# The opening of a fused attention and gated feed-forward kernel: half-image loads, line sums on other engines, row sums chunk by chunk, a new order

## The chip, the cores and the metric

The kernel runs on one core of one Trainium2 chip. The metric is the device time in microseconds of one execution of the whole program on that core; a lower time is better. Five kinds of work matter here: TensorE (PE in the profile; its weight loads are PEld), VectorE (DVE), ScalarE (ACT), GpSimd (POOL), and the transfers, which are issued by SyncE (SP), ACT or POOL and carried by 16 DMA engines.

## The reference, cut to what matters

```python
B, C, H, W, r = 4, 128, 384, 32, 4                  # four images
kv_pool = kv.reshape(B, H//r, r, W//r, r, C).mean(axis=(2, 4))
k = v = kv_pool.reshape(B, 768, C) @ w_sr           # 768 keys, which are the values too
s = q @ k.T / sqrt(C)                               # q: B x 12288 x 128
a = softmax(s)
x = a @ v                                           # 49152 rows of 128
out = (relu(x @ w_gate) * (x @ w_val)) @ w_out      # 128 -> 1536 -> 128
```

## The kernel before

The 49152 query rows are worked in 96 tiles of 512 rows, 24 tiles to an image. A tile goes through scores against its image's 768 keys (six chunks of 128), exponentials, the weighted sum of values, 24 projections to the 1536 inner columns (12 blocks called `v`, 12 called `g`), and 12 output products `o`. TensorE has eight PSUM banks of 128x512 for all results. The softmax division is done at the very end: the result of a tile is multiplied by the squared inverse of its row sums, which is right because the feed-forward part is of degree two in `x` and `relu` keeps the sign.

The order of all work is written out by hand as lists of words, and each engine executes what is given to it in program order. After the opening, which the list `OPENING` holds, tiles 4 to 95 run in a loop over `FIRST` (the first two rounds), `STEADY` and `DRAIN`. In a round the words `v1`, `y1`, `g1`, `h1` mean: the value projection of block 1 on TensorE, its copy to SBUF on ACT (`keep_value`), the gate projection on TensorE, and relu-and-multiply on VectorE (`gated`). `o1` is an output product, `s0` a score block, `e0` its exponential. The lists don't change for those rounds.

The opening does what has to come before the first round: the keys and values of image 0, and tiles 0 to 3 (the lead tiles) up to their weighted values and row sums, and the 24 projections of tile 0. Its words, each with its function:

- Image 0 comes in as three pairs of chunks. A chunk is 128 pooled pixels, and has four lines, each 128 partitions x 4 pixels x 128 channels in float32. The 16 pixels of a pooled pixel must be summed and the sum turned, channels to partitions. `a3`, `b3`, `c3` add whole lines (`sum_lines`, by the table `SUMS`), `p3` adds pixels 0,1 of that sum to 2,3 (`sum_pixels`), and `T3.0` turns line 0 of chunk 3 by TensorE transposes that add up in one bank: four of 128x128 for a line, two for `T3.p`, which turns what `p3` left. So each line is either summed elsewhere first or costs four transposes of its own.
- `kvT3` copies the bank to SBUF, `pj3` multiplies with `w_sr`, `key3` writes the keys, `vt3` and `val3` make the values from the keys by one transpose and a copy.
- `cast0`, `qt0`, `qT0` turn the queries of tile 0 (cast to float16, four transposes, copy); tiles 4 and 5 are turned by DMA (`qT4`, `qT5`).
- `S2.3` is the score product of tile 2 with chunk 3 and, in the same word, its exponential on ACT (line 345); `V2.3` adds the chunk to the tile's weighted values; `xT2` copies these.
- `U0` and `U1` are the row sums: `lead_sums` multiplies the exponentials with a block of ones for the four lead tiles at once, packed in four column groups (line 432). `U0` does five chunks, `U1` the sixth. `R` turns and inverts them on VectorE, and spreads them with 16 small copies on POOL.
- `v0.5` and `g0.5` are the projections of tile 0, each with its copy, or its relu-and-multiply, in the same word.
- `W0`, `W1`, `wo` are the loads of the feed-forward weights on POOL's queue; `gate22` holds them back until line 2 of chunk 5 is there. After the opening a second such copy (line 699) waits for block 11 of tile 0 before the query load of tiles 8 to 11.

The table `ENGINES` puts a word on ACT (`a`), POOL (`p`) or VectorE (`v`, also the default). A PSUM bank is taken by the next word that needs one in program order, from the bank that was freed longest ago; the instruction then waits for that bank's last reader. In the last eight words only six of the eight banks may be taken, as the rounds have just six for this use. The image and query loads are issued before all this, on SP, with two of the first lines on ACT's queue; the order is that of the calls at lines 592 to 600: pair 0, `w_sr`, queries 0 and 1, line 0 of pair 1, queries 2 and 3, lines 1 to 3 of pair 1, pair 2 (512 KB for each line of a pair), queries 5 and 4.

Of the kernel before, what the change touches and what calls it, by code (L numbers as in the profile page):

```python
# [11 lines left out]
AF = mybir.ActivationFunctionType  # L12
# [4 lines left out]
def kernel(  # L17
# [229 lines left out]
    def line(chunk, dh):  # L247
        return kv_in[0, chunk // 2][dh][:, chunk % 2]
# [88 lines left out]
    aTs, x_banks, x16s, xTs, rinvs = {}, {}, {}, {}, {}  # L337
    hTs, o_banks, o_sbs, vals = {}, {}, {}, {}

    def scores(k, jc):  # L340
        if k not in aTs:
            aTs[k] = work.tile([128, NJC, T], FP16, tag="aT", bufs=AT_BUFS, name="aT")
        s_ps = bank([128, T])
        nc.tensor.matmul(s_ps, kv16[:, k // NST, jc, 0:C], qT_of(k), start=True, stop=True)  # L344
# [79 lines left out]
        xTs[k] = work.tile([128, NS, 128], FP16, tag="xT", bufs=4, name="xT").rearrange("c s p -> c (s p)")  # L424
        copy_on(name, xTs[k], freed(x_banks.pop(k)))

    def lead_sums(chunks):
        if "sums" not in x_banks:
            x_banks["sums"] = bank([128, T])
        for jc in chunks:  # L430
            for k in range(LEAD):
                nc.tensor.matmul(  # L432
                    x_banks["sums"][32 * k : 32 * (k + 1), :], ones, aTs[k][:, jc, :],
                    start=jc == 0, stop=jc == NJC - 1, skip_group_check=True,
                    tile_position=(0, 32 * k),
                )
# [22 lines left out]

    def keep_value(k, fb):  # L460
        vals[k, fb] = work.tile([128, T], FP16, tag="val", bufs=6, name="val")
        (nc.vector.tensor_copy if k < LEAD - 1 and fb == 5 else nc.scalar.copy)(  # L462
            vals[k, fb], freed(proj_banks.pop(("v", k, fb)))
        )

# [126 lines left out]
    kv_load(0, 0, range(r), (nc.sync, nc.scalar))  # L592
    nc.sync.dma_start(w_sr_f32, w_sr)
    q_load_pair(0)
    kv_load(0, 1, range(1))
    q_load_pair(2)
    kv_load(0, 1, range(1, 4))
    kv_load(0, 2)
    q_load_tile(5)
    q_load_tile(4)  # L600
# [19 lines left out]
    freed(idle)  # L620

    gate = const.tile([128, 1], FP32)
    done = set()

    def open_step(word):
        head = "T" if word[0] == "T" else word.rstrip("0123456789.")
        at = [int(x) for x in word[len(head):].split(".") if x] if head != "T" else []
        if head in ("a", "b", "c"):
            j = at[0]
            x, y = SUMS[j][head]  # L630
            sum_lines(word, j, sums[j] if x == "s" else line(j, x), line(j, y))
        elif head == "p":
            sum_pixels(word, at[0])
        elif head == "r":
            c2 = pixels[at[0]]
            add(word, c2[:, 0], c2[:, 0], c2[:, 1])
        elif head == "T":
            j, part = word[1:].split(".")
            turn_add(
                int(j), line(int(j), int(part)) if part.isdigit() else  # L640
                pixels.pop(int(j))[:, 0 : 2 if part == "p" else 1],
            )
        elif head == "kvT":
            turned(word, at[0])
        elif head == "pj":
            project_chunk(at[0])
        elif head == "key":
            keep_keys(word, at[0])
        elif head == "vt":
            turn_chunk_values(at[0])  # L650
        elif head == "val":
            keep_chunk_values(word, at[0])
        elif head == "cast":
            q_cast(at[0])
        elif head == "qt":
# [153 lines left out]
```

## Time and profile before

| | |
|---|---|
| time, median of 3 runs | 1026.08 us (1025.98 to 1026.23) |
| the profiled execution: span from first to last instruction | 1024.5 us (the page gives no other time of it) |
| busy: PE, DVE, ACT, POOL | 1019.4, 861.8, 919.9, 524.8 us |
| opening on PE: first transpose, first word of the first round | 8.07 us, 36.44 us |
| granted TensorE clock | 1.000 |

Times are microseconds from the start of the span. A row of the timeline has the start, the length, engine, line, operation, what it writes and reads, and the count of a run of such instructions; in brackets the idle time ahead of it and what ended that. Matmuls are pipelined, so the length of one row is longer than the distance to the next: start to start is what an engine pays. A table by stage gives the busy time (and instructions) of PE, PEld, DVE, ACT and POOL in each stretch, the granted clock, the DMA share and GB/s.

### The profile page before, as it was taken

The page shows a single profiled execution, that of the slowest core. Times are in us where ns is not written, and L with a number is a line of the kernel's source. Part 1 is how long each engine was busy: PE and PEld are TensorE (multiplying, and loading weights), DVE is VectorE, ACT ScalarE, POOL GpSimd, SP SyncE. Part 2 cuts the span into 40 slices and gives each one's busy share as a digit, 9 for nine tenths or more (in the row PEclk, how much of TensorE's full clock was granted, in tenths as well). Part 3 has the DMA queues.
Part 4 walks back from the last instruction along what each step waited for, and adds up shares of the span by engine and source line. Part 5 has one row for each costly group of instructions (what it writes and reads, how often), then busy time and mean ns, then how long its engine had stood idle before and what let it go on. Part 6 is the DMA issues. An engine that isn't in the chain of part 4 may idle for free.

```text
span 1024.5 us, 17514 instructions
## 1 busy us (share of the span) xinstructions
PE 1019.4 (100%) x5048; PEld 489.5 (48%) x5048; DVE 861.8 (84%) x1432; ACT 919.9 (90%) x1931; POOL 524.8 (51%) x1308
## 2 busy tenths in 40 slices
PE   9999999999999999999999999999999999999998
PEld 5444444444444444444444444444444444444445
DVE  2888888888888888888888888888888888888888
ACT  5999999989999999899999999989999999999986
POOL 3588857344346586544434856654333543343342
DMA  9999999877998999869879899887686987867541
GB/s 330 159 173 184 176 183 159 151 131 120 139 184 168 189 186 164 143 115 146 128 126 211 160 180 194 157 138 134 118 139 108 145 134 119 129 115 123 102 87 45
DMA packets 475312, 153.49 MB, mean 150 GB/s; under 512 B 451536, under 2 KB 465360, under 8 KB 475216
## 3 DMA queue, kind: packets, MB, share of 16 engines
q1 hardware_dynamic: 453184, 126.08, 67.7%
q0 software_dynamic: 21600, 25.19, 15.9%
q10 hardware_dynamic: 432, 1.11, 0.3%
q8 instruction: 40, 0.66, 0.3%
q14 instruction: 56, 0.46, 0.1%
HBM read 53.94 MB, written 26.35 MB: 78 GB/s over the span
## 4 chain that ended last, share of the span: by engine, by line
PE 98%; DMA 1%; ACT 1%; SPq 0%; issue 0%
PE bank_ps L455 24%; PE bank_ps L468 24%; PE bank_ps L496 23%; PE bank_ps L401 12%; PE wide_ps L359 12%; DMA q<-in_q_dram 1%; PE bank_ps L482 1%; PE bank_ps L344 1%; PE bank_ps L418 1%; PE bank_ps L270 0%; PE wide_ps L302 0%; PE bank_ps L284 0%; ACT a L364 0%; ACT val L462 0%; PE bank_ps L432 0%
## 5 line engine op out<-in xcount | busy, mean ns | idle before, releaser
L476 DVE SCALAR_TENSOR_TENSOR hT<-bank_ps,val 128x512 f16<-128x512 f32 x1152 | 727.8, 680 | 105.4 <-PE bank_ps L468 83.7
L462 ACT CAST val<-bank_ps 128x512 f16<-128x512 f32 x1149 | 628.1, 595 | 45.4 <-PE bank_ps L455 24.9
L455 PE MATMUL bank_ps<-xT,wv 128*128 128x512 f16 x1152 | 420.5, 379 | 0.0
L468 PE MATMUL bank_ps<-xT,wg 128*128 128x512 f16 x1152 | 375.9, 379 | 0.0
L496 PE MATMUL bank_ps<-hT,wo 128*128 128x512 f16 x1116 | 348.4, 379 | 0.0
L364 ACT ACTIVATE a<-wide_ps 128x768 f16<-128x768 f32 x368 | 302.0, 821 | 44.0 <-PE wide_ps L359 43.9
L359 PE MATMUL wide_ps<-kv,qT 128*128 128x512 f16 x736 | 179.7, 326 | 0.1
L401 PE MATMUL bank_ps<-aT,kv 128*128 128x512 f16 x552 | 178.9, 379 | 0.0
L496 PEld LDWEIGHTS <-wo 128*128 128x128 f16 x1116 | 109.2, 98 | 131.9 <-issue 0.6
L468 PEld LDWEIGHTS <-wg 128*128 128x128 f16 x1152 | 112.7, 98 | 122.4 <-issue 0.2
L509 POOL TENSOR_TENSOR o_sb<-o_t,scale 128x512 f32<-128x512 f32 x89 | 93.2, 1047 | 145.9 <-issue 128.4
L455 PEld LDWEIGHTS <-wv 128*128 128x128 f16 x1152 | 112.7, 98 | 105.7 <-issue 1.2
L385 POOL COPY scale<-square 32x8 f32<-32x8 f32 x736 | 141.2, 192 | 28.6
L739 POOL DMA_DIRECT2D out_dram<-o_sb x216 | 134.8, 627 | 19.5 <-POOL o_sb L509 13.0
L378 POOL TENSOR_TENSOR square<-inverse 128x8 f32<-128x8 f32 x46 | 9.3, 202 | 255.6 <-DVE inverse L376 249.4
L359 PEld LDWEIGHTS <-qT 128*128 128x128 f16 x736 | 72.0, 98 | 87.1 <-issue 0.4
L409 DVE CAST xT<-bank_ps 128x512 f16<-128x512 f32 x92 | 63.6, 691 | 32.0 <-PE bank_ps L401 32.0
L401 PEld LDWEIGHTS <-kv 128*128 128x128 f16 x552 | 54.0, 98 | 65.1
L364 ACT ACTIVATION_READ_ACCUMULATOR a<-wide_ps 128x1 f32 x368 | 75.9, 206 | 0.0
L504 DVE STREAM_TRANSPOSE o_t<-bank_ps 128x512 f32<-128x512 f32 x93 | 65.4, 703 | 0.0
L144 POOL DMA_DIRECT2D q<-in_q_dram x84 | 46.7, 573 | 0.6 <-PE bank_ps L496 0.4
L237 POOL TENSOR_TENSOR s<-kv_in 128x512 f32<-128x512 f32 x36 | 45.1, 1284 | 0.7
(78 smaller groups left out, 204.9 us busy)
## 6 DMA issues: line engine op xcount, KB each, us to landing
kv_in<-in_kv_dram SPq DMA_DIRECT2D x42, 512.0 KB, 4.7
out_dram<-o_sb SPq DMA_DIRECT2D x177, 64.0 KB, 3.7
out_dram<-o_sb POOLq DMA_DIRECT2D x176, 64.0 KB, 4.2
q<-in_q_dram POOLq DMA_DIRECT2D x84, 128.0 KB, 5.8
aT<-a SPq DMA_TRANSPOSE x184, 4.3
kv_line<-in_kv_dram SPq DMA_DIRECT2D x4, 512.0 KB, 9.7
placed<-blocks SPq DMA_DIRECT2D x9, 128.0 KB, 2.7
kvT<-placed SPq DMA_DIRECT2D x36, 32.0 KB, 2.1
```

Source lines behind the costliest of these rows:

```text
L359: nc.tensor.matmul(s_ps[:, j0 * 128 : j1 * 128], qT, kv16[:, b, j0:j1, 0:C], start=True, stop=True)
L364: nc.scalar.activation(a16s[k][:, s, :], s_banks.pop(s)[:, 0:J], AF.Exp, scale=qk_scale, accum_out=a_sums[k // 2][:, k % 2, s : s + 1],)
L385: nc.gpsimd.tensor_copy(to[32 * b : 32 * (b + 1), :, :, j], squares[k // 2][32 * j : 32 * (j + 1)])
L401: nc.tensor.matmul(x_banks[k], kv16[:, k // NST, jc, C : 2 * C], aT[:, jc], start=first, stop=x_left[k] == 0,)
L455: nc.tensor.matmul(proj_banks["v", k, fb], wv16[:, fb * 128 : (fb + 1) * 128], xTs[k], start=True, stop=True,)
L462: (nc.vector.tensor_copy if k < LEAD - 1 and fb == 5 else nc.scalar.copy)(vals[k, fb], freed(proj_banks.pop(("v", k, fb))))
L468: nc.tensor.matmul(proj_banks["g", k, fb], wg16[:, fb * 128 : (fb + 1) * 128], xTs[k], start=True, stop=True,)
L476: nc.vector.scalar_tensor_tensor(hTs[k][:, fb, :], freed(proj_banks.pop(("g", k, fb))), 0.0, vals.pop((k, fb)), op0=ALU.max, op1=ALU.mult,)
L496: nc.tensor.matmul(o_banks[k], wo16[:, fb, :], hTs[k][:, fb, :], start=fb == 0, stop=fb == NFB - 1)
L504: nc.vector.transpose(o_t, freed(o_banks.pop(k)))
L509: nc.gpsimd.tensor_tensor(to, o_by, scale.to_broadcast([128, NS, 4, 32]), op=ALU.mult)
L739: queue.dma_start(*out_moves.pop())
```

## The change

Six things are changed, all in the opening:

1. The last pair of image 0 is loaded chunk by chunk: `kv_load` gets `half`, and `K4`, `K5` in the new list `LOADS` are four loads of 256 KB each, with rows of 2 KB in place of 4 KB. All other loads keep their order.
2. Lines 0 and 1 of every chunk are summed (`a`), and for chunks 2 to 5 line 2 is added too (`b`). Lines 2 and 3 of chunks 0 and 1 and line 3 of the others are still turned alone. That is 44 transposes of lines and sums in place of 62.
3. The row sums are made chunk by chunk (`U0` to `U5`), in six places of the list.
4. `S` and its exponential become two words (`S`, `E`), and so do `v` and its copy (`y`), `g` and its relu-and-multiply (`h`), so that other words may stand between.
5. `ENGINES`: ACT now has `kvT0`, `key1`, `cast1`, `qT2`, `val2`, `xT1`, `xT2` beside the exponentials and 11 of the 12 copies `y`; POOL has `a1`, `p0`, `b2`, `a4` and the casts of tiles 0, 4 and 5; VectorE has the rest, `y0.0` included.
6. A new `OPENING`, in which the last 12 words are held to six banks; `gate21` in place of `gate22` (line 1 of chunk 5).

```diff
-        key0:a val0:a a1:p kvT1:a key1:a val1:a key2:a val2:a a3:p b3:p p3:p kvT3:a val3:a
-        cast0:a cast1:a qT1:a cast3:a cast4:p cast5:p xT1:a xT3:a
+        cast4:p cast5:p a1:p p0:p kvT0:a cast0:p key1:a cast1:a qT2:a b2:p a4:p val2:a y0.0:v
+        xT1:a xT2:a
     """.split()
     OPENING = """
-        T0.1 T1.3 cast1 T0.3 cast0 T1.2 T0.2 a1 p1 T1.p T0.0 kvT1 kvT0 pj1 qt1 pj0 T2.0 qT1 a3
-        key1 cast3 qt0 cast2 vt1 qT0 key0 S1.1 qt2 qt3 qT2 val1 qT3 S1.0 S0.1 T2.1 S0.0 vt0 val0
-        V1.1 S2.0 b3 c3 S2.1 S3.0 S3.1 T2.2 V0.1 T2.3 V1.0 kvT2 V2.1 V0.0 p3 gate22 W0 W1 cast4
-        qT4 wo cast5 qT5 pj2 V2.0 T3.p T5.0 key2 vt2 kvT3 val2 pj3 key3 S0.2 T5.1 vt3 val3 S2.3
-        a4 S0.3 S1.2 S2.2 T5.2 V0.2 S3.2 b4 V2.3 T5.3 V0.3 c4 S1.3 kvT5 S3.3 pj5 p4 T4.p V1.2
-        key5 kvT4 V1.3 S0.5 pj4 key4 S2.5 vt5 val5 V2.2 S0.4 vt4 val4 S2.4 V0.5 V3.0 S1.4 V0.4
-        S3.4 xT0 S1.5 V2.5 V2.4 S3.5 xT2 v0.5 g0.5 U0 v0.2 U1 v0.0 R g0.2 v0.3 V1.4 V3.1 g0.0
-        v0.1 v0.4 V1.5 g0.3 v0.9 v0.11 g0.4 g0.9 V3.4 v0.8 v0.10 g0.1 xT1 g0.8 V3.5 v0.7 g0.11
-        V3.3 v0.6 V3.2 g0.10 xT3 g0.7 g0.6
+        a0 a1 p0 T1.2 p1 T0.2 T0.p T1.p T1.3 T0.3 kvT1 pj1 kvT0 pj0 cast0 key1 cast1 vt1 key0
+        qt0 val1 vt0 qt1 qT0 qT1 S0.1 S0.0 val0 S1.1 E0.1 S1.0 cast3 E0.0 V0.1 cast2 qt3 E1.1
+        V0.0 qt2 qT3 E1.0 V1.1 a3 S3.1 qT2 S3.0 V1.0 a2 E3.0 S2.1 S2.0 b3 b2 E3.1 V3.0 E2.1 p3
+        V3.1 E2.0 T3.p p2 T3.3 U0 T2.p kvT3 U1 pj3 a4 T2.3 key3 vt3 S1.3 kvT2 S0.3 val3 pj2
+        E1.3 b4 T4.3 E0.3 S3.3 key2 V1.3 p4 vt2 E3.3 S1.2 V0.3 a5 gate21 W0 W1 T4.p val2 S2.2
+        E1.2 S3.2 kvT4 V3.3 b5 E2.2 S0.2 pj4 V1.2 E3.2 p5 T5.3 key4 E0.2 T5.p S0.4 S3.4 kvT5
+        S2.4 E0.4 pj5 V3.2 E2.4 key5 vt4 U2 V0.2 val4 E3.4 S0.5 S3.5 vt5 E0.5 V0.4 V3.4 val5
+        S1.5 E3.5 V0.5 S2.5 E1.5 S2.3 xT0 V3.5 S1.4 E2.3 V1.5 xT3 v0.0 E2.5 v0.5 g0.3 y0.0 g0.0
+        y0.5 g0.5 U5 h0.0 E1.4 v0.1 v0.3 U3 y0.1 h0.5 U4 v0.6 y0.3 V2.0 cast4 qT4 wo cast5 qT5
+        R g0.6 v0.7 y0.6 V2.5 V1.4 y0.7 v0.8 h0.3 V2.4 V2.3 xT1 g0.7 h0.6 g0.1 y0.8 v0.2 g0.8
+        h0.7 v0.9 y0.2 V2.1 h0.8 v0.4 y0.9 g0.2 v0.11 h0.1 g0.11 y0.4 g0.4 v0.10 y0.11 h0.2
+        V2.2 g0.9 g0.10 y0.10 h0.4 xT2 h0.9 h0.11 h0.10
     """.split()
+    LOADS = "P0 w Q0 P1.0 Q2 P1.1 P1.2 P1.3 K4 K5 q5 q4".split()
...
-    SUMS = [{}, {"a": [0, 1]}, {}, {"a": [0, 1], "b": ["s", 2], "c": ["s", 3]}, {"a": [0, 1], "b": ["s", 2], "c": ["s", 3]}, {}]
+    SUMS = [{'a': [0, 1]}, {'a': [0, 1]}, {'a': [0, 1], 'b': ['s', 2]}, {'a': [0, 1], 'b': ['s', 2]}, {'a': [0, 1], 'b': ['s', 2]}, {'a': [0, 1], 'b': ['s', 2]}]
...
+            if half is not None:
+                own = slice(half * r * C, (half + 1) * r * C)
+                to, line_rows = to[:, own], line_rows[:, :, own]
+            queues[dh % len(queues)].dma_start(to, line_rows)
...
-        nc.scalar.activation(aTs[k][:, jc, :], freed(s_ps), AF.Exp, scale=qk_scale)
+
+    def exponentials(k, jc):
+        nc.scalar.activation(
+            aTs[k][:, jc, :], freed(score_ps.pop((k, jc))), AF.Exp, scale=qk_scale
+        )
...
-    def lead_sums(chunks):
+    def lead_sums(jc):
         if "sums" not in x_banks:
-            x_banks["sums"] = bank([128, T])
-        for jc in chunks:
-            for k in range(LEAD):
-                nc.tensor.matmul(
...
+            x_banks["sums"], x_count["sums"] = bank([128, T]), 0
+        x_count["sums"] += 1
+        for k in range(LEAD):
+            nc.tensor.matmul(
+                x_banks["sums"][32 * k : 32 * (k + 1), :], ones, aTs[k][:, jc, :],
+                start=x_count["sums"] == 1, stop=x_count["sums"] == NJC, skip_group_check=True,
+                tile_position=(0, 32 * k),
+            )
...
-        (nc.vector.tensor_copy if k < LEAD - 1 and fb == 5 else nc.scalar.copy)(
+        on_vector = ENGINES.get(f"y0.{fb}", "a") == "v" if k == 0 else k < LEAD - 1 and fb == 5
+        (nc.vector.tensor_copy if on_vector else nc.scalar.copy)(
...
-        elif head == "v":
-            value_proj(*at)
-            keep_value(*at)
-        elif head == "g":
-            gate_proj(*at)
-            gated(*at)
+        elif head in ("v", "y", "g", "h"):
+            {"v": value_proj, "y": keep_value, "g": gate_proj, "h": gated}[head](*at)
...
-        usable[0] = 8 if at < len(OPENING) - 8 else 6
+        usable[0] = 8 if at < len(OPENING) - 12 else 6
```

More of the change, by code (lines that the diff above doesn't have):

```diff
@@ L208, with kv_load @@
     kv_in = {}
-    def kv_load(b, pair, lines=range(r), queues=(nc.sync,)):
+    def kv_load(b, pair, lines=range(r), queues=(nc.sync,), half=None):
         if (b, pair) not in kv_in:
@@ L226, in kv_load @@
         for dh in lines:
-            queues[dh % len(queues)].dma_start(
-                parts[dh].rearrange("p h dw c -> p (h dw c)"), rows[dh]
-            )
+            to, line_rows = parts[dh].rearrange("p h dw c -> p (h dw c)"), rows[dh]
+            if half is not None:
+                own = slice(half * r * C, (half + 1) * r * C)
+                to, line_rows = to[:, own], line_rows[:, :, own]
+            queues[dh % len(queues)].dma_start(to, line_rows)
     s3s, kv_Ts, key_banks = {}, {}, {}
@@ L338 @@
     hTs, o_banks, o_sbs, vals = {}, {}, {}, {}
+    score_ps = {}
     def scores(k, jc):
@@ L342, in scores @@
             aTs[k] = work.tile([128, NJC, T], FP16, tag="aT", bufs=AT_BUFS, name="aT")
-        s_ps = bank([128, T])
+        s_ps = score_ps[k, jc] = bank([128, T])
         nc.tensor.matmul(s_ps, kv16[:, k // NST, jc, 0:C], qT_of(k), start=True, stop=True)
-        nc.scalar.activation(aTs[k][:, jc, :], freed(s_ps), AF.Exp, scale=qk_scale)
+    def exponentials(k, jc):
+        nc.scalar.activation(
+            aTs[k][:, jc, :], freed(score_ps.pop((k, jc))), AF.Exp, scale=qk_scale
+        )
     a16s, a_sums, squares, s_banks, x_left = {}, {}, {}, {}, {}
@@ L425, in lead_kept @@
         copy_on(name, xTs[k], freed(x_banks.pop(k)))
-    def lead_sums(chunks):
+    def lead_sums(jc):
         if "sums" not in x_banks:
-            x_banks["sums"] = bank([128, T])
-        for jc in chunks:
-            for k in range(LEAD):
[L432 to L436, printed above, removed]
+            x_banks["sums"], x_count["sums"] = bank([128, T]), 0
[6 more added lines that the diff above has]
+            )
     def lead_scales():
@@ L591 @@
     w_sr_f32 = const.tile([128, C], FP32)
[L592 to L600, printed above, removed]
+    for at, word in enumerate(LOADS):
+        n, _, dh = word[1:].partition(".")
+        lines = [int(dh)] if dh else range(r)
+        queues = (nc.sync, nc.scalar) if at == 0 else (nc.sync,)
+        if word == "w":
+            nc.sync.dma_start(w_sr_f32, w_sr)
+        elif word[0] == "P":
+            kv_load(0, int(n), lines, queues)
+        elif word[0] == "K":
+            kv_load(0, int(n) // 2, lines, queues, int(n) % 2)
+        elif word[0] == "Q":
+            q_load_pair(int(n))
+        elif word[0] == "q":
+            q_load_tile(int(n))
     warm = const.tile([128, 1], FP32)
@@ L622 @@
     gate = const.tile([128, 1], FP32)
-    done = set()
     def open_step(word):
@@ L640, in open_step @@
                 int(j), line(int(j), int(part)) if part.isdigit() else
+                sums.pop(int(j)) if part == "s" else
                 pixels.pop(int(j))[:, 0 : 2 if part == "p" else 1],
@@ L660, in open_step @@
             scores(*at)
-            done.add(tuple(at))
+        elif head == "E":
+            exponentials(*at)
         elif head == "V" and at[0] < LEAD:
@@ L666, in open_step @@
         elif head == "U":
-            lead_sums(range(at[0] * (NJC - 1), NJC - 1 + at[0]))
+            lead_sums(at[0])
         elif head == "R":
             lead_scales()
-        elif head == "v":
-            value_proj(*at)
-            keep_value(*at)
-        elif head == "g":
-            gate_proj(*at)
-            gated(*at)
+        elif head in ("v", "y", "g", "h"):
+            {"v": value_proj, "y": keep_value, "g": gate_proj, "h": gated}[head](*at)
         elif head == "W":
```

## The prediction

> **What bounds the kernel now.** I read the page's busy shares first, then the chain that ended last, then a table by stage, then the opening's timelines.
>
> ```profile
> PE 1019.4 (100%) x5048; PEld 489.5 (48%) x5048; DVE 861.8 (84%) x1432; ACT 919.9 (90%) x1931; POOL 524.8 (51%) x1308
> ...
> PE 98%; DMA 1%; ACT 1%; SPq 0%; issue 0%
> ```
>
> TensorE is busy for all but 5 us, and the chain is TensorE's: after the opening no round waits long enough to give anything back, so what the opening loses or gains is the result. The opening by stage:
>
> ```profile
> core 0: us, PE busy (x) PEld busy (x) DVE busy (x) ACT busy (x) POOL busy (x), PEclk, DMA share, GB/s
> 8.00:12.00 4.00, 3.60 (x29) 3.06 (x28) 0.38 (x2) 1.30 (x3) 0.00 (x0) 1.00 1.04 412
> 12.00:18.00 6.00, 6.00 (x52) 4.45 (x51) 2.54 (x6) 5.56 (x14) 2.90 (x3) 1.00 1.03 410
> 18.00:22.00 4.00, 4.00 (x29) 2.87 (x29) 1.58 (x3) 2.94 (x9) 1.76 (x5) 1.00 1.04 371
> 22.00:28.00 6.00, 6.00 (x34) 3.17 (x33) 3.43 (x10) 5.53 (x12) 1.88 (x4) 1.00 0.94 173
> 28.00:36.40 8.40, 8.40 (x56) 3.37 (x54) 7.78 (x15) 7.00 (x15) 6.54 (x22) 1.00 0.94 114
> ```
>
> To see here: TensorE fills every stretch from 12 us on, VectorE has room until 28 us and hardly any after, and the loads run at 410 GB/s to about 22 us. The transposes that the change removes are TensorE time now, but they are also what TensorE does while it waits for the first keys. Prices on TensorE come from starts:
>
> ```profile
> 14.43 0.60 PE L270 MATMUL bank_ps<-ident,kv_in 128*128 128x128 f32 x4
> 14.87 0.38 PE L344 MATMUL bank_ps<-qT,kv 128*128 128x512 f16 x1
> ...
> 28.06 0.38 PE L468 MATMUL bank_ps<-xT,wg 128*128 128x512 f16 x1
> 28.37 1.26 PE L432 MATMUL bank_ps<-aT,ones 128*32 128x512 f16 x20
> 29.56 0.39 PE L455 MATMUL bank_ps<-xT,wv 128*128 128x512 f16 x1
> 29.88 0.40 PE L432 MATMUL bank_ps<-aT,ones 128*32 128x512 f16 x4
> 30.21 0.39 PE L455 MATMUL bank_ps<-xT,wv 128*128 128x512 f16 x1
> ```
>
> Four transposes take 0.44 us (14.43 to 14.87), 0.11 each; a 128x512 product takes 0.216 (four score products in 0.86). A group of four row sums takes 0.22 (five in 1.1), and to enter and leave these costs 0.2 more each time: from the product at 29.56 to that at 30.21 is 0.65, less 0.22 and 0.22. The tail of the opening is VectorE's:
>
> ```profile
> 30.36 0.72 DVE L440 STREAM_TRANSPOSE sums_turned<-bank_ps 128x512 f32<-128x512 f32 x1 [0.44 <-PE bank_ps L432]
> 31.11 0.25 DVE L442 RECIPROCAL inverse<-sums_turned 128x16 f32<-128x16 f32 x1
> 31.40 0.17 DVE L444 TENSOR_TENSOR square<-inverse 128x16 f32<-128x16 f32 x1
> 31.49 6.69 DVE L476 SCALAR_TENSOR_TENSOR hT<-bank_ps,val 128x512 f16<-128x512 f32 x11
> 38.65 0.69 DVE L462 CAST val<-bank_ps 128x512 f16<-128x512 f32 x1 [0.47 <-PE bank_ps L455]
> ```
>
> `R` holds VectorE 1.15 us, then eleven `h` of 0.61 follow without a gap and end at 38.18. The list of banks shows why that matters: with six banks in use, `v5` of the first round takes the bank that the last of these `h` frees, and it starts at 38.23.
>
> **The change, part by part.**
>
> *Transposes.* 62 become 44: 18 x 0.11 = 1.97 us less work for TensorE.
>
> *Row sums.* The 24 products stay; the entries go from two to five (`U3` and `U4` adjoin on TensorE): 3 x 0.2 = +0.6 us.
>
> *The start.* TensorE now begins with `T1.2` and `T0.2`, which need line 2 of pair 0. It is SP's second load, issued at 1.49; the two landed 5.5 and 7.3 us after issue, so at 6.2 and 8.8. The first transpose is at 8.9 in place of 8.07 (`T0.1`). Twenty transposes follow, to 11.1. `a0` (VectorE), `a1`, `p0` (POOL, 1.26 + 0.73) and `p1` run from 6.3 to 8.4, under the wait.
>
> *First keys to `T3.p`.* From 11.1 `T2` no longer fills the waits. `pj1` at 11.1, `kvT0` on ACT, `pj0` 11.5, `key0` on VectorE 12.0 to 12.3 (a key copy starts 0.49 after its product, 23.41 to 23.90), `val1` 0.2, `qT0` 0.4 (its cast on POOL ends at 10.95, the query landed at 10.3): `S0.1` at 13.0, `S1.1` at 13.4 (13.33 before). Now ACT sets the pace: eight exponentials 0.54 apart (four in 2.14 us) with `qT2` between end at 18.3; before, the eighth ended at 18.14. The `V` words wait for them one by one. VectorE works `qT3` (14.8), `a3`, `a2`, `b3` (0.65 each), `p3` (0.4) in that order, to 17.6, so `T3.p` is at 17.7, not at 18.42. By then TensorE has issued 20 transposes, 2 `pj` (0.25), 4 `qt` (0.22), 2 `vt` (0.08), 14 products: 6.7 us of work in the 9.6 since 8.07, 2.9 idle. Before, it issued 42 transposes, 3 `pj` and the same rest, 9.4 us in 10.35, 0.95 idle. So +1.95 us of idle meet -1.97 of transposes.
>
> *From `T3.p` on.* More is left behind it: 24 transposes against 20 (+0.44), 4 `pj` against 3 (+0.25), the entries (+0.6). TensorE's last word comes 0.7 earlier by `T3.p` and 1.3 later by this: 37.0 in place of 36.44.
>
> *The tail.* From `T3.p` to the end of `U4` are 24 transposes (2.6), 4 `pj`, 4 `vt` (1.3), 34 products (7.3), the sums (1.3 + 5 x 0.2): 13.6 us, 31.3. With 0.2 for the result and 0.3 for small waits on banks `R` starts at 31.8 (30.36 before). Ten `h` are listed after it: 31.8 + 1.15 + 6.1 = 39.1. `v5` takes the bank of `h0.10`, the last: +0.9 on 38.18. ACT's last opening word ends near 37.8 (36.9 before), and that gap is the same. Nothing later gives it back: TensorE then runs unbroken to its one short wait at 55 us.
>
> *Loads.* SP issues eight loads of pair 2 in place of four, 4 x 0.6 us more, but its issue already waits for landings (the last query loads were issued one per landing, 1.28 apart), so this hides; the first weight load still waits for half of the remaining megabyte. Nothing shows the rate of 2 KB rows of an image. Bounds: the rate of the other loads, 410 GB/s, by which `K5` ends at 22.2 as pair 2 did; and that of the late 64 KB query loads with 2 KB rows, which landed 0.2 to 0.3 us apart beside the weights, 220 GB/s: 9.4 us in place of 5.1, or 26.5. I take the first: same queue, many loads in flight. `T5.3` is due at 24, so 1.8 us of cover; at the other end it waits 2.5 us.
>
> The Trainium skill's "DMA: Bandwidth & Descriptors" (Bandwidth) tells one to batch loads to 1 MiB and gives 341 GB/s there against 138 for 64 KB: midway, an estimate from that page, `K5` would end near 25.4 and cost 1.4. This trace moves 410 GB/s with 512 KB loads, several in flight.
>
> *TensorE's clock.* The fill products at the start took about 0.85 us a half, and 0.43 after some 4 us. A stretch with so many gaps could bring the slow clock back. The trace shows none: 8.07 to 13.3 is nearly all transposes and the next products still take 0.216, at granted clock 1.00.
>
> "TensorE: Matmul & The Clock Gate" (Part 4) says that transposes do not count as busy; by that rule the opening's first products should run at half speed before and after, 3 us more. The trace contradicts it.
>
> *Sum.* -1.97 + 0.6 + 1.95 is +0.6 on TensorE; VectorE's tail ends later, at +0.9, and decides. The span of the profiled execution, 1024.5, becomes 1025.4. The median is 1.6 above that span: 1027.0.
>
> **The rivals.**
> - *Faster: the sums come early.* Line 2 of pair 1 landed at 15.44; if VectorE takes `b3` then, `T3.p` could start at 16.6, 1.1 earlier: the tail ends at -0.2. With the idle wholly filled it would be -1.97 + 0.6 = -1.4, or 1024.7. VectorE's free time to 22 us speaks for it, the order `qT3 a3 a2 b3` against. It decides if `R` starts before 30.9.
> - *Loads of 2 KB rows are slow*: `T5.3` waits 2.5 us, together with the tail up to +2.5 (the waits overlap): 1028.6. Two thirds of the rate is enough to use up the cover.
> - *The clock falls* for one stretch of 4 us between 11 and 18: some 3 us of work doubles, idle takes half: +0.9 + 1.6, 1028.6.
> - *The change's aim fails in a mild way* (packing as before): within 0.3 of 1026.1.
>
> **How the numbers follow.** My forecast has 0.55, the early sums 0.15, no change 0.12, the loads 0.10, the clock 0.08. My forecast's own range is 1026.3 to 1027.9 (0.7 for `T3.p`, 0.3 for banks). Leaving out the deepest end of the first rival and the far ends of the two slow ones gives 1025.2 to 1028.4. A measurement here tells 0.2% (2.05 us) from no change: below 1024.03 only if more idle vanishes than the change adds (0.03); above 1028.13 most of the slow rivals (0.14); the rest, 0.83, lies between.
>
> **What would show it.** Right: first transpose near 8.9, a table by stage with TensorE 70 to 80% busy from 11 to 18, `R` near 31.8, the last `h` of tile 0 near 39.1, the first round's sixth projection waiting for it. Wrong: TensorE full from 12 us (first rival), a wait of `T5.3` on its load, or products 0.43 apart (clock). A wait on a word's engine order that I haven't followed, in the last 12 words above all, would make it wrong upward.

## The result, and the profile after

The changed kernel takes 1027.99 us (median of 21 runs, 1027.76 to 1032.86, three of them above 1029); the kernel before, on the same chips, 1026.56 us (21 runs, 1025.98 to 1027.3). The ratio is 1.0016, with a 95% interval of 1.0009 to 1.0023: about 1.4 us slower, which is within the 0.2% that was called no change. In several sets of runs, those of the kernel before included, single runs are 4 to 7 us longer, so times here are medians. The profiled execution took 1027.95 us with a span of 1026.1 us, so the span of the profiled executions grew by 1.6 us where +0.9 had been forecast. The kernel before's profiled execution, 1024.5, was a short one: over the 35 runs of it beside experiment 1 the median span is 1024.9, and over the 21 of the changed kernel it is 1026.1.

The page of the changed kernel, busy shares and then the chain that ended last, by engine:

```profile
PE 1019.5 (99%) x5030; PEld 487.5 (48%) x5030; DVE 868.1 (85%) x1445; ACT 918.1 (89%) x1923; POOL 526.3 (51%) x1309
...
PE 98%; DMA 1%; DVE 0%; ACT 0%; issue 0%; SPq 0%
```

TensorE issues 18 instructions fewer, yet its time without work rose from 5.1 us (span less busy) to 6.6. The table by stage of the changed kernel, columns as before (stretch; length, busy time of PE, PEld, DVE, ACT, POOL; granted clock; DMA share; GB/s):

```profile
core 0: us, PE busy (x) PEld busy (x) DVE busy (x) ACT busy (x) POOL busy (x), PEclk, DMA share, GB/s
8.00:12.00 4.00, 3.58 (x26) 2.76 (x24) 1.22 (x2) 0.53 (x3) 1.41 (x3) 1.00 1.05 414
12.00:18.00 6.00, 5.24 (x33) 2.42 (x32) 5.29 (x12) 5.05 (x11) 1.50 (x1) 1.00 1.03 399
18.00:22.00 4.00, 3.49 (x28) 2.27 (x29) 2.01 (x7) 0.33 (x1) 2.61 (x5) 1.00 1.07 372
22.00:28.00 6.00, 6.00 (x42) 3.75 (x41) 3.77 (x12) 5.37 (x12) 1.28 (x4) 1.00 1.02 182
28.00:36.40 8.40, 8.40 (x47) 3.37 (x46) 7.38 (x14) 7.95 (x16) 6.55 (x19) 1.00 0.95 111
```

From 12 to 22 us TensorE was full before; now 1.27 us of that is idle, and it issues 61 instructions there where it had issued 81. Short gaps don't show in these sums, as the modelled end of a product reaches past its start-to-start time: by starts, the 6.7 us of work that the forecast counted up to `T3.p` now lie in 10.44 us (8.07 to 18.51), so 3.7 us are idle, where 2.9 were forecast. VectorE went from 2.54 to 5.29 us of busy time between 12 and 18, some of it standing, as the rows below show. TensorE's clock stayed at 1.00 and the loads at about 400 GB/s. Most of what the table shows as idle is a single wait. The list of what TensorE waited for, in the whole execution (us in total, times, longest):

```profile
engine line waited for: us in total, times, longest us
PE bank_ps L633 <- POOL ident masks.py:199: 1.4, 1, 1.4
PE bank_ps L276 <- DVE kv_c L259: 1.1, 1, 1.1
PE bank_ps L276 <- DMA kv_in<-in_kv_dram: 0.4, 1, 0.4
```

The first row was there before. The last is the wait for line 2 of pair 0. The middle one, 1.1 us for VectorE's pixel sum, is `T3.p` waiting for `p3`. The timelines of VectorE, GpSimd and TensorE around it come next; the last two rows are the kernel before's, VectorE's `p1` and GpSimd's `b3`:

```profile
16.28 0.69 DVE L259 TENSOR_TENSOR kv_s<-kv_s,kv_in 128x512 f32<-128x512 f32 x1
17.00 1.37 DVE L259 TENSOR_TENSOR kv_c<-kv_s 128x256 f32<-128x256 f32 x1
...
16.50 1.59 POOL L259 TENSOR_TENSOR kv_s<-kv_s,kv_in 128x512 f32<-128x512 f32 x1 [5.55 <-DVE kv_s L259]
...
8.86 1.09 PE L276 MATMUL bank_ps<-ident,kv_in 128*128 128x128 f32 x8 [0.42 <-DMA kv_in<-in_kv_dram]
...
18.51 0.41 PE L276 MATMUL bank_ps<-ident,kv_c 128*128 128x128 f32 x2 [1.08 <-DVE kv_c L259]
...
7.66 0.43 DVE L253 TENSOR_TENSOR kv_c<-kv_s 128x256 f32<-128x256 f32 x1 [6.80 <-POOL kv_s L253]
...
15.56 1.26 POOL L253 TENSOR_TENSOR kv_s<-kv_s,kv_in 128x512 f32<-128x512 f32 x1
```

Read the second column. `p3` (the second row) is a 128x256 sum. Such a sum, `p1`, took VectorE 0.43 us in the profile before (`p3` itself was on GpSimd there); here it takes 1.37 us. Beside it lies `b2` on GpSimd, 16.50 to 18.09, which takes 1.59 us where such a sum took 1.26 before. `p3` ends 0.28 us after `b2`. Before, GpSimd's sums from 14.21 to 16.8 ran while VectorE made no sum, only copies from PSUM up to 14.73, and nothing was slowed.

The tail, VectorE's timeline of the changed kernel, TensorE's product that takes the bank of the last of the ten `h`, and the same product in the kernel before:

```profile
32.41 0.72 DVE L452 STREAM_TRANSPOSE sums_turned<-bank_ps 128x512 f32<-128x512 f32 x1 [0.20 <-PE bank_ps L444]
33.16 0.25 DVE L454 RECIPROCAL inverse<-sums_turned 128x16 f32<-128x16 f32 x1
33.45 0.17 DVE L456 TENSOR_TENSOR square<-inverse 128x16 f32<-128x16 f32 x1
33.54 6.25 DVE L489 SCALAR_TENSOR_TENSOR hT<-bank_ps,val 128x512 f16<-128x512 f32 x10
40.26 0.69 DVE L475 CAST val<-bank_ps 128x512 f16<-128x512 f32 x1 [0.47 <-PE bank_ps L467]
...
39.84 0.38 PE L467 MATMUL bank_ps<-xT,wv 128*128 128x512 f16 x1
...
38.23 0.38 PE L455 MATMUL bank_ps<-xT,wv 128*128 128x512 f16 x1
```

`R` starts at 32.41, the ten `h` run to 39.79 without a gap, and `v5` of the first round starts at 39.84; before it was 38.23. That difference, 1.61 us, is the whole difference of the two profiled spans: after it the two kernels run alike.

### The profile page after: what moved, and what is told of

Same layout as the page of the kernel before. It is cut to its first block, busy times and chain, and to the rows that moved or that the text cites. A ratio compares the mean times of both kernels' runs of the same rounds, so it can differ in the third digit from the quotient of the medians.

```text
span 1026.1 us, 17491 instructions
## 1 busy us (share of the span) xinstructions
PE 1019.5 (99%) x5030; PEld 487.5 (48%) x5030; DVE 868.1 (85%) x1445; ACT 918.1 (89%) x1923; POOL 526.3 (51%) x1309
## 4 chain that ended last, share of the span: by engine, by line
PE 98%; DMA 1%; DVE 0%; ACT 0%; issue 0%; SPq 0%
PE bank_ps L467 24%; PE bank_ps L481 24%; PE bank_ps L509 23%; PE wide_ps L371 12%; PE bank_ps L413 12%; DMA kv_in<-in_kv_dram 1%; PE bank_ps L495 1%; PE bank_ps L276 1%; PE bank_ps L352 0%; PE bank_ps L430 0%; PE wide_ps L308 0%; PE bank_ps L290 0%; PE bank_ps L444 0%; ACT a L376 0%; ACT val L475 0%
```

## The experiments

Two questions were open. What made `p3` slow, and is that the difference? And what are the other parts of the change worth: the transposes saved, the row sums chunk by chunk, the half loads, the tail? The theory at first was that the two sums on VectorE and GpSimd hold each other up, and that this costs most of the 1.6 us; its rival, that the five entries to the row sums or the idle time in place of the transposes cost it. Times are medians; "changed" is the changed kernel, "before" the kernel before on the same chip (1026.58 to 1026.74, against 1026.56 beside the changed kernel, which was not timed again; so a difference to it carries up to 0.2 us).

### 1. `b2` moved from GpSimd to VectorE, behind `p3`

```diff
-  ... cast1:a qT2:a b2:p a4:p val2:a ...
+  ... cast1:a qT2:a a4:p val2:a ...
-  ... S2.1 S2.0 b3 b2 E3.1 V3.0 E2.1 p3
+  ... S2.1 S2.0 b3 E3.1 V3.0 E2.1 p3 b2
```

> Changed kernel, but the sum b2 (line 2 added for chunk 2) is moved from POOL to VectorE, listed right behind p3. Theory (two engines in each other's way): in the changed kernel's trace p3 took 1.37 us and ended only after POOL's b2 had ended at 18.09, and its usual length is 0.42; without a POOL sum beside it p3 ends near 17.4, T3.p starts near 17.5 (18.51 in the changed kernel), R near 31.4 (32.41), and the time is 0.9 to 1.0 us below the changed kernel, about 1027.1 against 1026.5 of the kernel before. Rival (the tail decides alone, or p3 was late for its own queue): T3.p moves by less than 0.3 or the time by less than 0.3.

Measured: 1026.80 us (11 runs, 1026.66 to 1031.99), ratio to before 1.0003 (0.9989 to 1.0017); span 1025.0. VectorE's and TensorE's timelines of this run:

```profile
16.95 0.43 DVE L259 TENSOR_TENSOR kv_c<-kv_s 128x256 f32<-128x256 f32 x1
17.30 0.68 DVE L259 TENSOR_TENSOR kv_s<-kv_s,kv_in 128x512 f32<-128x512 f32 x1
18.02 0.42 DVE L259 TENSOR_TENSOR kv_c<-kv_s 128x256 f32<-128x256 f32 x1
...
17.53 0.41 PE L276 MATMUL bank_ps<-ident,kv_c 128*128 128x128 f32 x2
...
31.42 0.72 DVE L452 STREAM_TRANSPOSE sums_turned<-bank_ps 128x512 f32<-128x512 f32 x1 [0.20 <-PE bank_ps L444]
```

`p3` starts as before but takes 0.43 us, `T3.p` starts at 17.53, 0.98 us earlier, `R` at 31.42 (0.99 earlier), and the time falls by 1.2 us, the span by 1.1. VectorE does one sum more, and it is faster for that: `b2` costs VectorE 0.68 us, while on GpSimd it cost it 0.94 us of standing. The meeting of the two sums is 1.1 of the 1.6 us between the profiled spans. By median spans it is nearly all: 1026.1 in the changed kernel, 1025.0 here, 1024.9 in the kernel before.

### 2. All six row-sum groups at one place

```diff
-  T3.p p2 T3.3 U0 T2.p kvT3 U1 pj3 ... vt4 U2 V0.2 ... U5 h0.0 E1.4 v0.1 v0.3 U3 y0.1 h0.5 U4
+  T3.p p2 T3.3 T2.p kvT3 pj3 ... vt4 V0.2 ... h0.0 E1.4 v0.1 v0.3 U0 U1 U2 U5 U3 y0.1 h0.5 U4
```

> Changed kernel, but all six row-sum groups adjoin in the place of U3 and U4: one entry in place of five. Theory (each entry into the column groups and out of them costs TensorE 0.2 us that nothing hides, as it is busy without a gap from 18.5 us on): four entries less, R starts 0.8 us earlier, near 31.6, and the time falls by 0.6 to 0.8 us against the changed kernel. Rival (the entries lie in waits that stay): R moves by less than 0.2 and the time too.

Measured: 1027.53 us (1027.40 to 1028.24), ratio to before 1.0005 (0.9994 to 1.0017); `R` at 31.98, 0.43 earlier than in the changed kernel, and the time 0.46 less. That is half of what the prices of four entries (0.8) would give. `U0` and `U1` had stood in places where TensorE waits anyway: with them gone, TensorE waits 0.17 us for `pj3`. So the entries cost time, and part of it lay in waits.

### 3. Chunk 2 turned line by line again

`a2`, `b2`, `p2` are gone, so TensorE has ten transposes more, and VectorE and GpSimd have no sum for that chunk.

```diff
-  ENGINES  b2:p      SUMS[2] = {'a': [0, 1], 'b': ['s', 2]}
+  ENGINES            SUMS[2] = {}
-  kvT0 pj0 cast0 ... S3.1 qT2 S3.0 V1.0 a2 E3.0 S2.1 S2.0 b3 b2 E3.1 V3.0 E2.1 p3
-  V3.1 E2.0 T3.p p2 T3.3 U0 T2.p kvT3 U1 pj3 a4 T2.3 key3
+  kvT0 pj0 T2.0 cast0 ... S3.1 qT2 S3.0 T2.1 V1.0 E3.0 S2.1 S2.0 b3 E3.1 V3.0 E2.1 p3
+  T3.p V3.1 E2.0 T3.3 T2.2 U0 kvT3 pj3 U1 a4 T2.3 key3
```

> Changed kernel, but chunk 2 is turned line by line as before (T2.0 to T2.3, no a2, b2, p2), the transposes of lines 0 to 2 listed where TensorE waited. Theory (the removed transposes lay in waits for the first keys and exponentials, so they were worth nothing there, and the sums that replace them delay T3.p): ten transposes more, 1.1 us of TensorE work, yet T3.p starts near 17.1 (18.51), the first score of chunk 3 near 19.6 (21.25), and the time is 1.3 to 1.7 us below the changed kernel, near the kernel before. Rival (TensorE work counts wherever it lies): 1.1 us above the changed kernel, less what the freed VectorE gives.

Measured: 1027.75 us (1027.07 to 1034.64, six of twelve below 1027.6, three above 1032), ratio to before 1.0019 (1.0001 to 1.0036); span 1025.4, 0.7 less than the changed kernel's. `T3.p` came at 17.25, nearly as early as expected, but the first score of chunk 3 only at 20.31 (21.25 in the changed kernel, 20.27 in experiment 1 by the same 0.98), and `R` at 31.59. So the size was missed: from `T3.p` to chunk 3's projection it is 1.77 us, as in the changed kernel (1.80), but from there to the score 1.29 in place of 0.94, as the group `U1` (0.34) now stands behind the projection. What it does tell: against experiment 1, ten transposes more (1.1 us of TensorE) delay `R` by only 0.17 us. Most of that work fills time in which TensorE would wait. (The order around it differs too, and VectorE has three sums fewer, so 0.17 is not the price of the transposes alone.)

### 4. The last image pair by whole lines again

```diff
-    LOADS = "P0 w Q0 P1.0 Q2 P1.1 P1.2 P1.3 K4 K5 q5 q4".split()
+    LOADS = "P0 w Q0 P1.0 Q2 P1.1 P1.2 P1.3 P2 q5 q4".split()
```

> Changed kernel, but the last pair is loaded line by line for both chunks, as before (four loads of 512 KB). Theory (the half loads are hidden, and help a little at most): the last line of chunk 4 is there near 22.2 in place of about 19.5, which T4.3 needs at 21.95, so T4.3 waits 0.3 us; the sum a4 is not late; the time is 0 to 0.3 us above the changed kernel. Rival (2 KB rows are slow and part of the loss): the time falls by 0.3 us or more.

Measured: 1028.54 us (1027.96 to 1029.31), ratio to before 1.0015 (1.0003 to 1.0027); span 1026.4. TensorE's timeline shows the price:

```profile
22.36 0.63 PE L276 MATMUL bank_ps<-ident,kv_line 128*128 128x128 f32 x4 [0.45 <-DVE kv L297]
```

`T4.3` starts at 22.36 behind a gap of 0.45 us; with the half loads it starts at 21.95 and has no gap. The row names VectorE's writing of chunk 2's keys, but in the changed kernel `T4.3` ran ahead of that (21.95 against 22.21); the last load of this pair was issued at 11.3 and landed 10.9 us later, near 22.2, and is the likely cause. By the profiled executions the half loads gain 0.3 us (the span and the last `h`) to 0.45 (the gap); the ratios to before, 1.0016 with them and 1.0015 here, don't tell the two kernels apart. Their 2 KB rows cost nothing that shows: from 8 to 18 us the loads run at 399 to 414 GB/s either way.

### 5. Experiment 1, with the inverse of the row sums made behind the last `h`

The tail of the opening looked like VectorE's. Here `R` only turns the sums; the reciprocal, the square and GpSimd's 16 copies come in a word `I` at the end of the list.

```diff
-  V2.2 g0.9 g0.10 y0.10 h0.4 xT2 h0.9 h0.11 h0.10
+  V2.2 g0.9 g0.10 y0.10 h0.4 xT2 h0.9 h0.11 h0.10 I
   nc.vector.transpose(turned ...)
+  x_banks["turned"] = turned
+
+  def lead_inverse():
+      turned = x_banks.pop("turned")
       nc.vector.reciprocal ...
```

> The kernel with b2 on VectorE (e1), and of R only the turn of the sums stays in its place; its reciprocal and its square, 0.43 us of VectorE, are a word of their own behind the last h of tile 0. Theory (the last h of tile 0, which frees the bank for the sixth projection of the first round, sets the end of the opening): the last h ends 0.43 earlier, that projection starts 0.43 earlier, and the time falls by 0.4 against e1, to about 1026.4. Rival (TensorE's or ScalarE's own work sets it, VectorE's tail is only beside): no change, within 0.1 of e1.

Measured: 1033.73 us (1031.46 to 1035.14), ratio to before 1.0061 (1.0045 to 1.0077), span 1030.0. Both halves of the expectation failed. VectorE's timeline:

```profile
32.12 1.25 DVE L493 SCALAR_TENSOR_TENSOR hT<-bank_ps,val 128x512 f16<-128x512 f32 x2
33.80 4.93 DVE L493 SCALAR_TENSOR_TENSOR hT<-bank_ps,val 128x512 f16<-128x512 f32 x8 [0.43 <-PE bank_ps L485]
```

With 0.4 us of work taken from it, VectorE waits 0.43 us for TensorE's gate projection, and the last `h` ends where it did (38.73, and 38.66 in experiment 1). So the tail is set by TensorE and VectorE together, not by VectorE alone. And the loss, 5.0 us of span between this profiled execution and that of experiment 1, is elsewhere. GpSimd's timeline (first three rows), what TensorE waited for after 50 us (fourth), and the table by stage from 100 to 120 us (last two):

```profile
39.16 3.65 POOL L463 COPY lead_scale<-square 32x16 f32<-32x16 f32 x16 [7.41 <-DVE square L460]
42.88 0.19 POOL L720 CAST gate<-hT 128x1 f32<-128x1 f16 x1
43.42 2.17 POOL L148 DMA_DIRECT2D q<-in_q_dram  x4 [0.35 <-issue]
...
PE bank_ps L413 <- DMA aT<-a: 3.2, 2, 2.9
...
100.00:110.00 10.00, 7.11 (x30) 2.88 (x28) 5.31 (x11) 5.50 (x12) 8.83 (x29) 0.84 1.29 181
110.00:120.00 10.00, 10.00 (x49) 4.74 (x48) 7.97 (x13) 8.72 (x19) 6.45 (x11) 0.99 0.90 193
```

The 16 copies now stand ahead of the query load of tiles 8 to 11 in GpSimd's order, and it is issued at 43.42 instead of 38.76. SP's turn of these queries moves from 49.19 to 53.86, and the DMA turns of the probabilities on the same queue come late for TensorE: 3.2 us of waits, and in the 10 us with the long one the granted clock is 0.84, which costs, by an estimate, 1.1 to 1.6 us more (0.16 of the 7.11 busy or of all 10). Together that is 4.3 to 4.8 of the 5.0 us. That the copies' place is the cause was then only argued; experiment 8 tests it. The way from the late load over SP's queue to TensorE is read from the order of these rows and was not tested by itself.

### 6. Experiment 5, with `U2` and `U5` beside `U3` and `U4`

```diff
-  vt4 U2 V0.2 ... g0.5 U5 h0.0 E1.4 v0.1 v0.3 U3 y0.1 h0.5 U4
+  vt4 V0.2 ... g0.5 h0.0 E1.4 v0.1 v0.3 U2 U5 U3 y0.1 h0.5 U4
```

> e5, and the row-sum groups of chunks 2 and 5 moved to adjoin those of 3 and 4; those of chunks 0 and 1 stay, as they stood in waits. Theory (an entry costs 0.2 us where TensorE is full, and nothing in a wait): two entries less, R and the time 0.4 earlier than e5, about 1026.0. Rival (entries are worth only half, as when all six were put together): 0.2.

Measured: 1032.78 us (1030.68 to 1036.2), ratio to before 1.006 (1.0041 to 1.0079). `R` came at 31.15, 0.33 earlier than in experiment 5, but 0.16 of that was there at `T3.p` (17.42 against 17.58), ahead of the groups that moved; and the same late wait (3.8 us) hid whatever the rest was worth. The expectation failed for the reason of experiment 5.

### 7. Chunk 3 ahead of chunk 2, alone and with the last two

Chunk 3's sums go before chunk 2's, all sums but `a1` and `p0` go to VectorE, and the first scores of chunk 3 go ahead of the transposes of chunk 2; first without the edits of 5 and 6, then with them.

```diff
-  ENGINES  b2:p a4:p
+  ENGINES
-  V1.1 a3 S3.1 qT2 S3.0 V1.0 a2 E3.0 S2.1 S2.0 b3 b2 E3.1 V3.0 E2.1 p3
-  V3.1 E2.0 T3.p p2 T3.3 U0 T2.p kvT3 U1 pj3 a4 T2.3 key3 vt3 S1.3 kvT2 S0.3 val3 pj2
-  E1.3 b4 T4.3 E0.3 S3.3 key2 V1.3 p4 vt2 E3.3 S1.2 V0.3 a5 gate21 W0 W1 T4.p val2 S2.2
+  V1.1 a3 S3.1 qT2 S3.0 V1.0 E3.0 S2.1 S2.0 b3 E3.1 V3.0 E2.1 p3
+  T3.p V3.1 a2 E2.0 T3.3 kvT3 pj3 U0 b2 key3 vt3 S1.3 val3 S0.3 p2 T2.p E1.3 T2.3 U1 kvT2 E0.3
+  S3.3 pj2 a4 V1.3 E3.3 b4 T4.3 key2 V0.3 p4 vt2 S1.2 a5 gate21 W0 W1 T4.p val2 S2.2
```

> The changed kernel with the sums b2 and a4 on VectorE and the sums of chunk 3 ahead of those of chunk 2 there (a3 b3 p3 and then a2 b2 p2), the scores of chunk 3 listed ahead of the rest of chunk 2. Theory (what is left of the loss beside the blocked sum is VectorE's queue of sums, in which a2 stands ahead of b3): T3.p starts near 16.9 (18.51 changed, 17.53 in e1), the first score of chunk 3 near 19.0 (20.27 in e1), R near 30.6 and the time 0.6 to 0.9 us below e1, about 1026.0. Rival (TensorE has the same work behind it whatever the order): no better than e1.

> All of e5, e6 and e7 together. Theory: their gains add, as they lie one behind the other on the way to the last h of tile 0: 0.4, 0.4 and 0.6 to 0.9 below e1: 1025.2, below the kernel before by 1.2 us or so. Rival (an earlier end of VectorE's tail uncovers ScalarE's copies or TensorE): they add to less than 1 us.

Measured: 1028.32 us alone (1028.09 to 1030.12), ratio to before 1.0009 (0.9996 to 1.0023), and 1033.94 with the others (1.0037 to 1.0079). Both expectations failed. The profiled execution of the first is the longest of its eleven (1030.12, span 1028.3; the median span is 1026.3), but its opening fits the median: the last `h` ends at 39.82, 0.03 after that of the changed kernel. Alone, `T3.p` came at 17.10 and the first score of chunk 3 at 19.49, but `R` at 32.58, later than in the changed kernel (32.41): expected was 30.6. What was late next is VectorE's queue: chunk 2's last sum came at 19.83, its copy at 21.21 after 0.97 us in which VectorE had to wait, and `b4` at 22.14 (20.63 in experiment 1). The gain on one chunk was paid by the next two. The second kernel adds to that the late waits of experiment 5 (4.4 us in its profiled execution).

### 8. Experiment 5, with the 16 copies behind the query load

```diff
   nc.gpsimd.tensor_copy(gate, hTs[0][:, NFB - 1, 0:1])
   q_load(2)
+  lead_spread()
```

> e5 again (reciprocal and square of R behind the last h), but POOL makes the 16 copies of R only after it has issued the query load of tiles 8 to 11. Theory (e5 lost 7 us because the copies, then late, stood ahead of that load in POOL's order: it was issued at 43.4 in place of 38.8, SP's turn of these queries at 53.9 in place of 49.2, and TensorE waited 2.9 us for a transposing transfer between 100 and 200 us): the load is issued near 38.7, SP's turn near 49, no wait of TensorE on such a transfer, and the time is that of e1, 1026.8, within 0.2, as VectorE's last h was no earlier in e5 than in e1. Rival (the late scales themselves did it): above 1030 again.

Measured: 1026.91 us (1026.78 to 1032.56), ratio to before 1.0002 (0.9987 to 1.0017). The load is issued at 38.71, SP's turn starts at 48.36, and TensorE's late waits shrink to 0.2 us. So the place of 3.65 us of small copies ahead of one load was worth nearly 7 us, and the shorter VectorE tail nothing: the time is that of experiment 1.

### 9. Experiment 1, with `U2` and `U5` beside `U3` and `U4`

The edit of the list is that of experiment 6, on top of experiment 1's:

```diff
-  vt4 U2 V0.2 ... g0.5 U5 h0.0 E1.4 v0.1 v0.3 U3 y0.1 h0.5 U4
+  vt4 V0.2 ... g0.5 h0.0 E1.4 v0.1 v0.3 U2 U5 U3 y0.1 h0.5 U4
```

> The kernel with b2 on VectorE (e1), and the row-sum groups of chunks 2 and 5 adjoining those of 3 and 4, with R left whole. Theory (an entry costs TensorE 0.15 to 0.2 us where it is full; in e6 against e5 two entries less moved R by 0.33): R near 31.1 (31.42 in e1), time 0.3 below e1, about 1026.5. Rival (the gain is lost in the tail): as e1, 1026.8.

Measured: 1026.97 us (1026.61 to 1028.56), ratio to before 1.0000 (0.9990 to 1.0010). `R` came at 31.25 and `v5` at 38.55, each 0.17 us earlier than in experiment 1, and the profiled execution gives 0.4 us back in one wait for a DMA turn. No gain that can be told from nothing; and two entries less moved `R` by 0.17 us, about the 0.17 that is left of the 0.33 in experiment 6.

### 10. Experiment 9, with chunk 0 turned line by line

```diff
-  a0 a1 p0 T1.2 p1 T0.2 T0.p T1.p T1.3 T0.3      SUMS[0] = {'a': [0, 1]}
+  a1 T0.0 T0.1 T1.2 p1 T0.2 T1.p T1.3 T0.3       SUMS[0] = {}
```

> e9, and chunk 0 turned line by line as before (no a0, p0), with lines 0 and 1 first, while TensorE would wait for line 2 of pair 0. Theory (a transpose in a wait costs nothing; the wait from the fill's end to 8.86 takes most of eight of them): first transpose at 8.1 in place of 8.86, pj1 0.1 to 0.2 earlier than 11.21, R the same amount earlier, time 0.1 to 0.2 below e9. Rival (ScalarE's exponentials, which start at 13.45 after the query's cast, set the pace): no change.

Measured: 1027.38 us (1026.58 to 1028.62), ratio to before 1.0004 (0.9994 to 1.0015). In the profiled execution the fill products at the start held TensorE until 8.74 (their row lasts 7.54 us; in experiment 1 it lasts 6.20), so the six transposes more could not use the wait for line 2. `pj1` started at 11.69 rather than 11.17 (experiment 9), everything was some 0.5 us late, and a sum on VectorE met one on GpSimd again. VectorE's row, and then GpSimd's:

```profile
18.53 1.37 DVE L259 TENSOR_TENSOR kv_c<-kv_s 128x256 f32<-128x256 f32 x1
...
18.33 1.29 POOL L259 TENSOR_TENSOR kv_s<-kv_line 128x512 f32<-128x512 f32 x1 [7.25 <-DMA kv_line<-in_kv_dram]
```

This is `p2` beside `a4`: 1.37 us again. In experiment 1, `p2` had started at 18.02, 0.13 us ahead of `a4`, and taken 0.42. At the start of the same run, with `p0` and `a0` gone, `p1` takes 0.43 us and `a1` 1.26; in the changed kernel, beside `p0` and `a0`, they take 0.93 and 1.76. So the sum that starts second pays, whichever engine it is on, and 0.2 us decide. What chunk 0's sums are worth this run can't say: the profiled execution, 1028.30 us, is one of the longer of twelve, and five lie below 1027.0.

### 11. Experiment 9, with `a4` on VectorE too

```diff
-  ENGINES  a4:p      ... pj3 a4 T2.3 key3
+  ENGINES            ... pj3 T2.3 a4 key3
```

> e9, and the sum a4 moved to VectorE too, listed behind the first transposes of chunk 2's last line, where VectorE waited 1.1 us. So no POOL sum runs beside VectorE's sums after 9 us. Theory (VectorE's sum of two SBUF operands and POOL's sum block each other; in e10, where all was 0.5 later, p2 met a4 and took 1.37 us, and in e1 and e9 it began only 0.13 before a4): p3 and p2 take 0.42 each, R is near 31.1 as in e9, the time 1026.4 to 1026.8, and its runs lie close together. Rival (p2's 1.37 in e10 came from something else, or VectorE has no room for a4): a long p2 or p3 again, or a later R and a time above 1027.

Measured: 1027.48 us (1026.86 to 1031.63), ratio to before 1.0014 (1.0004 to 1.0023). The landmarks came as expected: `p3` and `p2` take 0.42 us each, `R` comes at 31.12 and the span of the profiled execution is 1024.9. The time did not: it is 0.7 us above the upper end. In this execution 2.6 us lie outside the span, where experiment 1 had 1.8; over the eleven runs the medians are 2.25 outside and a span of 1025.1, no shorter than experiment 1's 1025.0. What makes that outer part longer stays open.

No version beats the kernel before. Experiments 1, 8 and 9 come within 0.4 us of it, which is inside the noise.

## Why the prediction was right

The forecast, 1027.0 and "same", was right in its mechanism and a little small: the 1027.99 measured lies within its outer range (1025.2 to 1028.4) and just above its own (1026.3 to 1027.9). Against the 21 runs of the kernel before, 1026.56 in place of the 1026.08 of three, the change is +1.4 where +0.9 was forecast. By its own steps:

| step | forecast | measured |
|---|---|---|
| first transpose, waiting for line 2 of pair 0 | 8.9 | 8.86 |
| `pj1`, `S0.1` | 11.1, 13.0 | 11.21, 13.04 |
| end of the eight exponentials | 18.3 | 17.98 |
| `T3.p` | 17.7 | **18.51** |
| `T3.p` to the end of `U4` | 13.6 | 13.7 |
| `R` | 31.8 | 32.41 |
| last of the ten `h`, then `v5` | 39.1 | 39.79, 39.84 |
| profiled span | 1025.4 | 1026.1 |

- The step that failed is the duration of `p3`. It was priced at 0.4 us, from a row of a profile in which GpSimd stood still; it took 1.37 beside `b2`. With `b2` away (experiment 1) `T3.p` comes at 17.53, `R` at 31.42, and the last `h` at 38.66: each a little ahead of the forecast's. So the span missed by +1.1 for this, less 0.4 that the rest of the sum had too much; that the second made up for part of the first was luck. The sums at the start, `a1` and `p1`, stood in the same way (1.76 and 0.93 us) and ended at 9.08 rather than 8.4, but that lay under the wait for line 2 of pair 0 and the transposes behind it.
- That rest: the waits on banks (0.3 in the sum) did not come, and the exponentials ended 0.3 earlier.
- Saved transposes against idle time, forecast at -1.97 and +1.95: right as far as the runs go. Without the meeting of the sums (experiment 1) the changed order with 18 transposes fewer is at the time of before, and in experiment 3 ten transposes more delay `R` by 0.17 us, not by 1.1.
- Row-sum entries, 0.2 each: experiment 2 gave 0.43 us for four that moved and experiment 9 0.17 for two, so about half of the price lay in waits. The +0.6 was an upper end.
- "VectorE's tail decides": only in part. Experiment 5 took 0.4 us from VectorE and TensorE's projections came last at once.
- The early-sums rival fell: `R` came at 32.41, not before 30.9; and where `T3.p` did come early (17.10, experiment 7), `R` was no earlier. The loads rival fell: the loads ran at about 400 GB/s, the last of `K5`, issued at 16.7, landed 5.8 us later, near 22.5, and `T5.3` had no wait on its load; experiment 4 shows no loss by the half loads. (240 GB/s, the middle of the two rates that the prediction quotes, would have put the end of `K5` at 25.8 and not at the 25.4 given there.) The clock rival fell: 1.00 in every stretch of the opening, in spite of a gap of 1.08 us. What the prediction calls a contradiction shows less than that: from 8.07 to 11.69 the kernel before has only transposes, then also projections, and the clock didn't fall; whether transposes alone keep it up for longer no run shows. The mild rival, within 0.3 us of the time before, fell: it is +1.4.
- Of the 1.0 us between forecast and median, 0.7 is the span; the rest lies outside it (1.85 us in the changed kernel's profiled execution; the 1.6 taken was the median of three runs less the span of one execution).

## What to carry to other kernels

Before a sum is moved to GpSimd, look at what VectorE does in the same microsecond: a duration from a profile in which the other engine stood still is a lower end, and where VectorE alone is done sooner with both sums, both belong there. Work taken from the bound engine is a gain only where it isn't what that engine does while it waits; here 18 transposes fewer brought nothing. And an edit's place in a queue can count more than its length: 3.65 us of copies ahead of one load cost nearly 7 us, 60 us later.

## What was not expected of the hardware

- Two sums with both operands in SBUF, one on VectorE and one on GpSimd, didn't run side by side in any row of the opening here. The one that starts second stands until the other ends: 0.43 us became 1.37 (`p3`, and `p2` in experiment 10) and 0.93 (`p1`) on VectorE, each ending 0.28 or 0.29 us after GpSimd's sum; 1.26 became 1.76 (`a1`), 1.59 (`b2`), 1.33 and, in experiment 1, 1.41 (`a4`) on GpSimd, each ending 1.12 or 1.13 us after VectorE's. It isn't only sums: GpSimd's one-column copy `gate21`, which holds the weight loads back, takes 0.19 us in the changed kernel and 0.60 in experiment 1, where VectorE's `b4` began 0.13 us ahead of it. The Trainium skill's page "SBUF — State Buffer" (Who interferes with whom) states this: the two engines share a pair of ports under an exclusive lock, and a VectorE instruction with two SBUF inputs contends with a GpSimd instruction that reads SBUF, whichever came first. The rows of this case agree with it.
- During one wait of 2.9 us of TensorE (experiment 5, up to 107.26 us) the granted clock fell: 0.50 from 107 to 110 us, with 128x512 products 0.43 us apart, and 1.00 again from 110.5, where they are 0.22 apart. Gaps of up to 1.5 us in the opening (1.48 in experiment 5) left it at 1.00.
- The ten fill products at the start, the same in all kernels, ended between 7.4 and 9.0 us in the profiled executions (their rows last 6.04 to 7.62 us from 1.36). `p2` and `a4`, 0.13 us apart in experiment 1, leave less room than that; whether they meet in some executions of one and the same kernel no run shows.
